# A fused attention and two-layer MLP kernel: selection rows made ahead of the decay, queries loaded once, another transfer price in the planner

## The chip, the cores and the metric

The kernel runs as one program on one core of one Trainium2 chip. The metric is device time in microseconds (us). The core has TensorE (PE in the profile; its weight loads, which overlap its matmuls, are PEld), VectorE (DVE), ScalarE (ACT), GpSimd (POOL) and SyncE (SP). SP issues every transfer of this kernel, in program order, and all of them share the core's 16 DMA engines.

## The reference, cut to what matters

```python
# q, k, v: [4, 8, 576, 64]; f: [4, 8, 576] in 0.8 .. 1.0
cum = np.cumsum(np.log(np.clip(f, 0.0001, 1.0)), axis=-1)
scores = q @ k.T / 8 + cum[..., :, None] - cum[..., None, :]   # causal mask
attn = softmax(scores) ;  x = (attn @ v) -> [2304, 512]
# layer 1: 512 -> 1024 -> 512
h = x @ w_in ;  solu = h * softmax(h) ;  ln = layernorm(solu) * g_ln
x = ln @ w_out
# layer 2: 512 -> 2048 -> 512
h = maximum(x @ w2_in, 0) ;  out = (h * h) @ w2_out
```

All tensors are float32. The kernel keeps that precision by splitting every large operand into a rounded high part and a low part (the difference), so that one product is three matmuls, or two with stacked rows.

## The kernel before

**Stages.** The 576 query rows of each of the 4 batches are cut into tiles of 128 rows (and one of 64), 20 tiles in all. For each tile and each of the 8 heads, `head` (L467) computes scores z (two matmuls, L488), their row minimum with the causal mask (DVE, L509), the exponential (ACT, L523) and the transposes of the result (PE, L543, copied out by a helper at L303), and `mix` (L549) multiplies two heads by v (PE, L564). When 128 rows of x are complete, `first` (L771) runs layer 1 on them (L786 to L788, then L863 and, in `out1`, L727 to L729) between later attention heads. Layer 2 runs at the end in blocks of 384 rows (`step`, L1044: L1059 to L1061 and L1089 to L1091). The weights come as raw words and are split on chip by `convert` (L619): a load (L629), then ACT L643, a scaling (L305 or L307), DVE L647 and L651, POOL L657, a rounding copy (L303 or L307) and the low part (L661, DVE or POOL). The weights of layer 1 are converted during the first attention tiles, those of layer 2 after the last one.

**The decay inside the score product.** A score is a product over 128 rows of `K1` and `Q1` plus one over 80 rows of `K2` and `Q2`. Rows 64 to 79 of `K2` hold the cumulated log of f (high and low part, 8 heads each), put there by small transfers (`auxrows`, L429). The same rows of `Q2` select the head with ones and zeros: `picks` (L398, L405) makes them once for each of the four `Q2` buffers, from the identity matrix alone. `picks` for the two buffers of the first tile carry the priority -6.9e6. For the first tile `c0` (the first 128 columns of the cumulated log, in two parts) goes straight into `K2`; the later tiles read it from a copy in DRAM, `cumd`.

**Operands.** `load` (L373) fetches k and q of a tile, for each half j of the heads, as 128 rows in which the 64 rows of the head dimension stand twice. `prep_k` (L409) rounds k into `K1` and writes its low part into `K2` (L421, on DVE or POOL, whichever the planner takes). `prep_q` (L443) writes the scaled, rounded q into `Q2` rows 0 to 63 and `Q1` rows 64 to 127, and its low part into `Q1` rows 0 to 63 (DVE, L456). k and q have one raw buffer for each half (`KN`, `QN`), so the load of the next tile waits until the last reader of its buffer is done.

**What sets the order.** Each step is given to a planner (`Plan`, L23) with a cost for each engine that may run it, a priority, and what it reads and writes. `Plan.lay` (L94) then lays out all steps before the program is built: of the steps that could start within 20 ns of the earliest it takes the one with the lowest priority number, chooses the engine, and so fixes the order on every engine's queue and on SP. On the chip an engine takes its queue strictly in this order; a step whose input is late holds all that stand behind it. The planner treats transfers as a sixth engine: 256 KB cost 800 ns, and `LAT` adds 910 to 1290 ns until the reader can start. `port=True` marks DVE steps that the planner keeps apart from POOL steps.

## Time and profile before

| | us |
|---|---|
| median of 3 timed runs | 898.15 (897.89 to 899.88) |
| the profiled execution, its own time | 895.01 |
| its span, first to last instruction | 892.9 |
| PE busy in the span | 841.4 (94%) |
| DVE, ACT, POOL busy | 459.4, 496.5, 294.1 |

The profiled execution lies 2.9 us below the lowest of the timed runs; 2.1 us of its time lie outside its span. Busy time of PE counts pipelined matmuls, so it is time in which PE had something in flight. The stages in time: attention and the conversion of the layer 1 weights to about 100 us, attention and layer 1 to about 450 us, conversion of the layer 2 weights beside the first blocks of layer 2 to about 570 us, and the rest of layer 2.

### The profile page before, as it was taken

Reading aid. Unit: us, or ns where it says so; the run is one execution under the profiler, and the core shown is the slowest. Engines: PE = TensorE matmul, PEld = TensorE weight load, DVE = VectorE, ACT = ScalarE, POOL = GpSimd, SP = SyncE. Lnnn points to the kernel's source line nnn. Section 1 sums busy time; section 2 is a strip of 40 time slices with the busy share of each in tenths; the row PEclk is TensorE's granted clock in tenths of the full one; section 3 lists DMA queues with packets and bytes.
Section 4 is the critical chain, followed back from the end, with each engine's and each line's share of the span. In section 5 each row is a group of like instructions: output and inputs, shape, how many; then the busy total and the mean of one; then the engine's idle time right before and its main releaser. Section 6 shows DMA issues by size and latency. Waiting matters only on the chain.

```text
span 892.9 us, 15185 instructions
## 1 busy us (share of the span) xinstructions
PE 841.4 (94%) x5360; PEld 728.5 (82%) x5360; DVE 459.4 (51%) x1139; ACT 496.5 (56%) x1286; POOL 294.1 (33%) x379
## 2 busy tenths in 40 slices
PE   3788899999999999999996999999999999999998
PEld 2556777888888888888875988899999999999997
DVE  6878666655655556655676789722222222222221
ACT  6889878666866667756675777523322222222222
POOL 6567756223521236211387788700000000000000
PEclk9979999999999999999998999999999999999999
DMA  6723335222511125010544644105002002000000
GB/s 219 233 86 126 106 108 157 83 59 66 171 48 37 59 67 165 29 42 24 162 145 132 223 140 131 48 1 177 36 0 72 36 1 71 36 1 1 36 0 36
DMA packets 55499, 75.26 MB, mean 84 GB/s; under 512 B 7456, under 2 KB 35104, under 8 KB 55424
## 3 DMA queue, kind: packets, MB, share of 16 engines
q1 hardware_dynamic: 55424, 74.30, 26.6%
q8 instruction: 42, 0.69, 0.3%
q14 instruction: 33, 0.27, 0.1%
HBM read 59.91 MB, written 14.30 MB: 83 GB/s over the span
## 4 chain that ended last, share of the span: by engine, by line
PE 77%; DVE 9%; DMA 5%; ACT 5%; issue 3%; POOL 2%; SPq 0%; POOLq 0%; DVEq 0%; ACTq 0%
PE pp L1059 6%; PE pp L1061 6%; PE pp L1060 6%; PE z L488 6%; PE pp L543 6%; PE xo L564 6%; PE pp L727 3%; PE hp L786 3%; PE hp L787 3%; PE hp L788 3%; PE pp L728 3%; PE pp L729 3%; PE hp L1089 2%; PE hp L1090 2%; PE hp L1091 2%
## 5 line engine op out<-in xcount | busy, mean ns | idle before, releaser
L1067 ACT ACTIVATE q<-pp 128x384 f32<-128x384 f32 x96 | 47.1, 491 | 223.1 <-PE pp L1061 221.0
L1070 DVE CAST q<-q 128x384 fp32r<-128x384 f32 x96 | 42.1, 438 | 243.4 <-PE xo L1091 92.3
L523 ACT ACTIVATE adj<-z,st 64x288 f32<-64x288 f32 (+9 forms) x192 | 94.9, 497 | 31.0 <-DVE st L509 29.3
L488 PE MATMUL z<-k,q 128*128 128x256 f32 (+17 forms) x384 | 95.1, 347 | 12.7 <-DVE q L456 9.1
L509 DVE CUSTOM_DVE_ANT_0 z<-z,maskb 128x128 f32<-128x128 f32 (+8 forms) x144 | 65.6, 464 | 52.8 <-PE z L488 49.9
L303 ACT COPY pt<-pp 128x384 f32<-128x384 f32 (+5 forms) x170 | 67.9, 420 | 39.0 <-PE pp L543 37.3
L543 PE MATMUL pp<-ident,adj 128*128 128x128 f32 (+1 forms) x480 | 78.7, 280 | 8.7 <-ACT adj L523 8.4
L727 PE MATMUL pp<-ln,woh 128*128 128x256 f32 x288 | 84.2, 292 | 2.3 <-ACT pt L303 2.3
L728 PE MATMUL pp<-ln,wol 128*128 128x256 f32 x288 | 80.8, 280 | 0.0
L729 PE MATMUL pp<-ln,woh 128*128 128x256 f32 x288 | 80.7, 280 | 0.0
L543 PEld LDWEIGHTS pp<-ident,adj 128*128 128x128 f32 (+1 forms) x480 | 52.8, 143 | 30.2 <-ACT adj L523 19.4
L488 PEld LDWEIGHTS z<-k,q 128*128 128x128 f32 (+3 forms) x384 | 58.4, 188 | 19.7 <-ACT q L305 7.9
L564 PE MATMUL xo<-pt,vn 128*64 128x128 f32 (+1 forms) x960 | 70.3, 278 | 3.8 <-ACT pt L303 3.1
L564 PEld LDWEIGHTS xo<-pt,vn 128*64 128x64 f32 x960 | 50.6, 140 | 23.6 <-issue 11.8
L786 PE MATMUL hp<-wih,xl 128*128 128x512 f32 x144 | 61.5, 427 | 2.2 <-ACT hp L825 1.8
L727 PEld LDWEIGHTS pp<-ln,woh 128*128 128x128 f32 x288 | 55.1, 191 | 5.3 <-ACT pt L303 2.6
L787 PE MATMUL hp<-wil,xh 128*128 128x512 f32 x144 | 57.2, 397 | 0.5 <-POOL wil L661 0.5
L788 PE MATMUL hp<-wih,xh 128*128 128x512 f32 x144 | 57.2, 397 | 0.0
L728 PEld LDWEIGHTS pp<-ln,wol 128*128 128x128 f32 x288 | 55.0, 191 | 0.5
L729 PEld LDWEIGHTS pp<-ln,woh 128*128 128x128 f32 x288 | 54.8, 190 | 0.0
L1069 ACT ACTIVATE q<-q 128x384 f32<-128x384 f32 x96 | 50.4, 525 | 2.5
L307 POOL TENSOR_SCALAR q<-qn 64x512 fp32r<-64x512 f32 (+1 forms) x43 | 28.0, 652 | 55.3 <-PE z L488 50.0
(470 smaller groups left out, 2233.5 us busy)
## 6 DMA issues: line engine op xcount, KB each, us to landing
x2d<-xc SPq DMA_DIRECT2D x72, 128.0 KB
kn<-in_k_dram SPq DMA_DIRECT2D x32, 256.0 KB
qn<-in_q_dram SPq DMA_DIRECT2D x32, 256.0 KB
vn<-in_v_dram SPq DMA_DIRECT2D x20, 256.0 KB
ln<-x2d SPq DMA_DIRECT2D x24, 192.0 KB
out_dram<-pt SPq DMA_DIRECT2D x18, 256.0 KB
pt<-in_moe_w_in_dram SPq DMA_DIRECT2D x17, 256.0 KB
ln<-in_moe_w_in_dram SPq DMA_DIRECT2D x8, 512.0 KB
```

The costliest lines, as they stand in the source:

```text
L303: nc.scalar.copy(dst(), src())
L488: nc.tensor.matmul(dst, lhsT=ql[0:r, p, 0:m], rhs=rhs, start=(g == 0), stop=(g == 1))
L509: nc.vector.tensor_tensor_reduce(out=z, in0=z, in1=maskb[0:m, o : o + e - a], scale=1.0, scalar=st[0:m, 0:1] if y else 3e38, op0=ALU.add, ...
L523: nc.scalar.activation(out=adj[0:m, c[1] : c[2]], in_=Z[c[0]][0:m, 0 : c[2] - c[1]], func=AF.Exp, bias=st[0:m, low : low + 1], scale=-1.0, ...
L543: nc.tensor.transpose(at(sk)[:, (c - g) * m : (c - g + 1) * m], adj[0:m, zc : zc + P], ident[0:m, 0:m])
L564: nc.tensor.matmul(XO[own[j], p, off : off + m], lhsT=VN[vslot[b, c]][:, (2 * p + j) * D : (2 * p + j + 1) * D], rhs=pts[j][:, c * m : (c ...
L727: nc.tensor.matmul(px, lhsT=woh[:, fc, w], rhs=lo, start=(fc == 0), stop=False)
L728: nc.tensor.matmul(px, lhsT=wol[:, fc, w], rhs=hi, start=False, stop=False)
L729: nc.tensor.matmul(px, lhsT=woh[:, fc, w], rhs=hi, start=False, stop=(fc == KF - 1))
L786: nc.tensor.matmul(HP[:, c], lhsT=XL[i][:, cc, :], rhs=wih[:, cc, w], start=(cc == 0), stop=False)
L787: nc.tensor.matmul(HP[:, c], lhsT=XH[i][:, cc, :], rhs=wil[:, cc, w], start=False, stop=False)
L788: nc.tensor.matmul(HP[:, c], lhsT=XH[i][:, cc, :], rhs=wih[:, cc, w], start=False, stop=(cc == KC - 1))
```

## The change

1. **Picking rows.** `picks` for the first tile's buffers gets priority -9.05e6, ahead of the steps on f (-9e6); that for the second tile's buffers goes from 5000 to 14000.
2. **First tile's parts.** The clip and the scan of the other 448 columns of f get -6.5e6 in place of -9e6 + 1. The low part of k of the first tile may run on DVE alone, no longer on POOL.
3. **Queries.** q is laid out once in DRAM: one load of 128 rows holds half 0 in rows 0 to 63 and half 1 in rows 64 to 127, into a single buffer `qn`. The steps of `prep_q` read the half that they need from it, across rows; the low part of half 1 takes the rounded value from `Q1`. The number of steps of `prep_q` is as before. The freed buffer (`q3`) serves layer 2 in place of the second `qn`.
4. **Planner.** 256 KB cost 1140 ns (230 GB/s; the other transfers in proportion), 500 ns more pass from a transfer to its reader, and a POOL step is not taken when a DVE step that needs the shared port, with a lower priority number by more than `DUE`, would start before the POOL step ends and lose more by waiting than POOL would.

```diff
-        dma=dict(pe=1000, dve=950, act=910, pool=950, dma=1290),
+        dma=dict(pe=1500, dve=1450, act=1410, pool=1450, dma=1790),
...
+                if e == "pool":
+
+                    end = c[0] + c[1].eng[e]
+                    x = [
+                        max(free["dve"], y.rdy["dve"]) for y in avail["dve"]
+                        if y.port and len(y.eng) == 1 and y.eng["dve"] and y.prio < c[1].prio - DUE
+                    ]
+                    if any(y < end and end - y > (y - c[0]) * WORTH for y in x):
+                        continue
...
-    QN = [new(f"qn{i}", [DM]) for i in range(2)]
+    QN = new("qn", [DM])
...
     def load_q(n, prio):
-        load("qn", QN, q, n, prio + 1)
+        T = tiles[n]
+        m, o = T["m"], HH * T["q0"]
+        pl.add(
+            dict(dma=1140 * m / P), lambda: nc.sync.dma_start(QN[:, 0 : HH * m], q[T["b"], :, o : o + HH * m]), prio + 1,
+            writes=["qn"],
+        )
...
-        s = pl.add(dict(dve=602, pool=1252) if i else dict(dve=602), fn, -6.9e6 if i == 0 else 5000, ["ident"], [("qa", i, j)], port=True)
+        s = pl.add(dict(dve=602, pool=1252) if i else dict(dve=602), fn, -9.05e6 if i == 0 else 14000, ["ident"], [("qa", i, j)], port=True)
...
-                dict(dve=67 + 1.045 * HH * m, pool=119 + 2.213 * HH * m), lo, prio + 2 * j, [("kn", j)] + hk, lk,
+                dict(dve=67 + 1.045 * HH * m, pool=119 + 2.213 * HH * m) if n else dict(dve=67 + 1.045 * HH * m),
+                lo, prio + 2 * j, [("kn", j)] + hk, lk,
...
-        for j in range(2):
+        raw = QN[:, 0 : HH * m].rearrange("p (h s) -> p h s", s=m)
+        for j, src in enumerate(own):
...
-            def lo(q1=q1, q2=q2, raw=raw):
+            def lo(src=src, q1=q1, hi=(q1 if j else q2)):
                 nc.vector.scalar_tensor_tensor(
-                    out=q1[LO, :, 0:m], in0=raw[LO], scalar=SC, in1=q2[LO, :, 0:m].bitcast(F32), op0=ALU.mult,
+                    out=q1[LO, :, 0:m], in0=raw[src], scalar=SC, in1=hi[src, :, 0:m].bitcast(F32), op0=ALU.mult,
...
-        pl.add(dict(dma=max(350, 2.844 * n)), words, prio - AHEAD, writes=[lk, hk])
+        pl.add(dict(dma=4.45 * n), words, prio - AHEAD, writes=[lk, hk])
...
-            ), -9e6 + y, ["f"], [("f", y)],
+            ), -9e6 + y * 2.5e6, ["f"], [("f", y)],
...
-            dict(dve=200 + 2 * n), scan, -9e6 + y, [("lf", y), "ones"] + ["cu0", ("xh", 0, 0)] * y, [f"cu{y}"]
+            dict(dve=200 + 2 * n), scan, -9e6 + y * 2.5e6, [("lf", y), "ones"] + ["cu0", ("xh", 0, 0)] * y, [f"cu{y}"]
```

The program is laid out anew, so the order shows what the numbers did. All names below: `adj` holds f and its logs at the start, `xh0` the two parts of c0, `q100`/`q200` and `q101`/`q201` are `Q1`/`Q2` of the first tile for half 0 and 1, `k20`/`k21` is `K2`, `ln` the raw words of w_in.

DVE at the start of the program, before:

```order
L1158 TENSOR_SCALAR adj0_30_97<-adj0_30_97 32x128
L1158 TENSOR_SCALAR adj0_30_97<-adj0_30_97 32x448
L1151 SCALAR_TENSOR_TENSOR adj2_32_99<-e_49_116,adj1_31_98 32x128
L1170 CAST xh0_45_112<-adj2_32_99 32x128
L1173 TENSOR_TENSOR xh0_45_112<-adj2_32_99,xh0_45_112 32x128
L1151 SCALAR_TENSOR_TENSOR adj2_32_99<-e_49_116,adj2_32_99,adj1_31_98 32x448
L456 SCALAR_TENSOR_TENSOR q100_12_79<-qn0_22_89,q200_16_83 64x512
L456 SCALAR_TENSOR_TENSOR q101_13_80<-qn1_23_90,q201_17_84 64x512
L405 TENSOR_TENSOR q200_16_83<-ident_0_67 16x512
L405 TENSOR_TENSOR q201_17_84<-ident_0_67 16x512
L1183 TENSOR_TENSOR pt1_51_174<-adj2_32_99,pt0_50_166 32x576
```

and after the change:

```order
L416 TENSOR_TENSOR q200_16_83<-ident_0_67 16x512
L416 TENSOR_TENSOR q201_17_84<-ident_0_67 16x512
L1175 TENSOR_SCALAR adj0_29_96<-adj0_29_96 32x128
L1175 TENSOR_SCALAR adj0_29_96<-adj0_29_96 32x448
L1168 SCALAR_TENSOR_TENSOR adj2_31_98<-e_48_115,adj1_30_97 32x128
L1187 CAST xh0_44_111<-adj2_31_98 32x128
L1190 TENSOR_TENSOR xh0_44_111<-adj2_31_98,xh0_44_111 32x128
L1168 SCALAR_TENSOR_TENSOR adj2_31_98<-e_48_115,adj2_31_98,adj1_30_97 32x448
L432 TENSOR_TENSOR k20_10_77<-kn0_20_87,k10_8_75 64x4x128
L468 SCALAR_TENSOR_TENSOR q100_12_79<-qn_22_89,q200_16_83 64x512
L432 TENSOR_TENSOR k21_11_78<-kn1_21_88,k11_9_76 64x4x128
L468 SCALAR_TENSOR_TENSOR q101_13_80<-qn_22_89,q101_13_80 64x512
L1200 TENSOR_TENSOR pt1_50_175<-adj2_31_98,pt0_49_162 32x576
```

The picking rows (L405, now L416) went from behind the queries' low parts to the front of the queue, ahead of the clip of f; the two low parts of k (L432), which POOL held before, now stand between the scan of the 448 columns and the first row minimum.

SP, from the first load of w_in (`ln`) to the third, before:

```order
L629 DMA ln0_50_168<-in_moe_w_in_dram 128x1024
L1130 DMA cumd_59<-pt0_50_166 32x576
L379 DMA kn0_20_87<-in_k_dram 128x512
L379 DMA qn0_22_89<-in_q_dram 128x512
L1130 DMA cumd_59<-pt1_51_174 32x576
L379 DMA kn1_21_88<-in_k_dram 128x512
L379 DMA qn1_23_90<-in_q_dram 128x512
L395 DMA vn1_25_92<-in_v_dram 128x512
L629 DMA ln0_50_168<-in_moe_w_in_dram 128x1024
L629 DMA ln1_51_234<-in_moe_w_in_dram 128x1024
```

and after the change:

```order
L644 DMA ln0_49_166<-in_moe_w_in_dram 128x1024
L1147 DMA cumd_59<-pt0_49_162 32x576
L388 DMA kn0_20_87<-in_k_dram 128x512
L1147 DMA cumd_59<-pt1_50_175 32x576
L396 DMA qn_22_89<-in_q_dram 128x512
L388 DMA kn1_21_88<-in_k_dram 128x512
L406 DMA vn1_24_91<-in_v_dram 128x512
L644 DMA ln0_49_166<-in_moe_w_in_dram 128x1024
L644 DMA ln1_50_238<-in_moe_w_in_dram 128x1024
```

One q load in place of two stands between the first and the second load of w_in.

ACT, in the second half of the first tile, around the second chunk of w_in (the `ACTIVATE ln` from L643, now L658), before:

```order
L523 ACTIVATE adj1_31_98,su0_40_107<-z0_117,st0_36_103 128x128
L523 ACTIVATE adj2_32_99,su0_40_107<-z1_118,st1_37_104 128x128
L303 COPY pt0_33_100<-pp2_123 128x128
L303 COPY pt1_34_101<-pp0_121 128x128
L643 ACTIVATE ln0_50_168<-ln0_50_168 128x512
L305 ACTIVATE ln0_50_168<-ln0_50_168 128x512
L303 COPY pt2_35_102<-pp1_122 128x128
L523 ACTIVATE adj0_30_97,su0_40_107<-z0_117,st2_38_105 128x128
L523 ACTIVATE adj1_31_98,su0_40_107<-z1_118,st3_39_106 128x128
```

and after the change:

```order
L538 ACTIVATE adj2_31_98,su0_39_106<-z1_117,st1_36_103 128x128
L314 ACTIVATE q110_14_81<-qn_22_89 64x512
L312 COPY pt0_32_99<-pp2_122 128x128
L312 COPY pt1_33_100<-pp0_120 128x128
L538 ACTIVATE adj0_29_96,su0_39_106<-z0_116,st2_37_104 128x128
L312 COPY pt2_34_101<-pp1_121 128x128
L658 ACTIVATE ln0_49_166<-ln0_49_166 128x512
L312 COPY pt0_32_99<-pp2_122 128x128
L314 ACTIVATE q111_15_82<-qn_22_89 64x512
L538 ACTIVATE adj1_30_97,su0_39_106<-z1_117,st3_38_105 128x128
```

Two of the exponentials (`adj`) stood behind the second chunk of w_in before, one does now, and two scalings of q (L314) moved here from POOL.

## Rows read from the trace of the kernel before

**Rows 1.** The page, part 1: busy us, share, instructions of PE.

```profile
PE 841.4 (94%) x5360; PEld 728.5 (82%) x5360; DVE 459.4 (51%) x1139; ACT 496.5 (56%) x1286; POOL 294.1 (33%) x379
```

**Rows 2.** Stages: busy us by engine, granted clock, DMA share, GB/s.

```profile
0.00:20.00 20.00, 7.40 (x29) 5.14 (x30) 14.03 (x29) 12.44 (x32) 14.32 (x25) 1.00 0.68 212
20.00:40.00 20.00, 15.30 (x79) 10.81 (x79) 14.82 (x36) 17.43 (x47) 10.17 (x11) 1.00 0.73 228
40.00:60.00 20.00, 15.17 (x75) 10.92 (x76) 17.17 (x32) 16.36 (x40) 11.30 (x8) 0.66 0.44 140
...
100.00:150.00 50.00, 46.83 (x388) 38.11 (x387) 32.86 (x101) 37.97 (x124) 30.86 (x42) 0.97 0.42 126
...
300.00:350.00 50.00, 50.00 (x430) 41.41 (x431) 28.10 (x92) 35.63 (x110) 21.93 (x27) 1.00 0.32 100
...
450.00:500.00 50.00, 39.12 (x216) 34.24 (x215) 37.49 (x74) 32.46 (x86) 39.44 (x52) 0.93 0.40 128
```

**Rows 3.** What PE waited for, 0 to 150 us: total, times, longest.

```profile
PE z L488 <- DVE q L456: 9.1, 2, 8.0
...
PE z L488 <- DVE q L405: 1.7, 1, 1.7
```

**Rows 4.** Timeline of the start: start, us, engine, line, operation, [idle before].

```profile
1.50 0.29 POOL masks.py:199 TENSOR_SCALAR_AFFINE_SELECT ident<-ident 128x128 f32<-128x128 f32 x1
...
5.26 4.30 POOL L421 TENSOR_TENSOR k<-kn,k 64x512 fp32r<-64x512 f32 x2
...
6.15 2.29 DVE L456 SCALAR_TENSOR_TENSOR q<-qn,q 64x512 fp32r<-64x512 f32 x2
...
8.45 3.10 DVE L405 TENSOR_TENSOR q<-ident 16x512 fp32r<-16x512 f32 x2
...
11.58 0.75 DVE L1183 TENSOR_TENSOR pt<-adj,pt 32x576 fp32r<-32x576 f32 x1
12.26 0.28 DVE L509 CUSTOM_DVE_ANT_0 z<-z,maskb 128x128 f32<-128x128 f32 x1
...
12.87 0.68 DVE L405 TENSOR_TENSOR q<-ident 16x512 fp32r<-16x512 f32 x1
```

**Rows 5.** The chain of waits, 0 to 27 us: start us, us, what.

```profile
2.72 0.67 DVE adj L1158 x2
...
4.72 1.50 DVE adj L1151
...
14.16 7.00 DMA ln<-in_moe_w_in_dram
...
23.96 1.38 DVE wil L661
...
26.08 0.78 PE z L488 x2
```

**Rows 6.** Timeline of ACT, up to 22 us.

```profile
5.55 0.63 ACT L305 ACTIVATE q<-qn 64x512 fp32r<-64x512 f32 x1
...
18.21 0.42 ACT L303 COPY pt<-pp 128x128 f32<-128x128 f32 x2
...
21.19 0.66 ACT L643 ACTIVATE ln<-ln 128x512 f32<-128x512 f32 x1 [2.56 <-DMA ln<-in_moe_w_in_dram]
```

**Rows 7.** Timeline of SP, three of its issues.

```profile
14.16 0.91 SPq L629 DMA_DIRECT2D ln<-in_moe_w_in_dram  x2
...
29.55 0.46 SPq L1130 DMA_DIRECT2D gcol<-in_moe_g_ln_dram  x1
35.22 0.34 SPq L379 DMA_DIRECT2D kn<-in_k_dram  x1
```

**Rows 8.** Stages 14 to 21.2 us and 41.5 to 55.5 us.

```profile
14.00:21.20 7.20, 6.26 (x26) 3.95 (x25) 3.33 (x12) 4.11 (x18) 4.33 (x5) 1.00 0.85 266
...
41.50:55.50 14.00, 10.76 (x46) 7.82 (x43) 13.12 (x24) 12.00 (x27) 8.62 (x6) 0.51 0.45 145
```

**Rows 9.** Timeline of PE: the last of the eight L786 of the first tile.

```profile
64.67 0.40 PE L786 MATMUL hp<-wih,xl 128*128 128x512 f32 x1
```

More of the change, by code (lines that the diff above doesn't have):

```diff
@@ L371, in tile_kernel, with load_k @@
     vslot = {}
-    def load(nm, dst, src, n, prio):
+    def load_k(n, prio):
         T = tiles[n]
@@ L768, in out1 @@
                 wk = [("x2d", a, cc, 2 * blk + r) for r in range(2)]
-                pl.add(dict(dma=365), store(a), prio, [(nm, i, r) for r in range(2)], wk)
+                pl.add(dict(dma=570), store(a), prio, [(nm, i, r) for r in range(2)], wk)
     def first(x):
@@ L977, in tile_kernel @@
     small = [f"vn{i}" for i in range(NV)] + [f"q{a}{i}{j}" for a in (1, 2) for i in range(2) for j in range(2)]
-    small += ["kn0", "kn1", "qn0", "qn1"]
+    small += ["kn0", "kn1", "qn", "q3"]
     skeys = {f"vn{i}": [("vn", i)] for i in range(NV)}
     for i in range(2):
-        skeys[f"kn{i}"], skeys[f"qn{i}"] = [("kn", i)], [("qn", i)]
+        skeys[f"kn{i}"] = [("kn", i)]
         for j in range(2):
@@ L1111, in step @@
                 pl.add(
-                    dict(dma=728), lambda o=o, r0=r0: nc.sync.dma_start(out[r0 : r0 + P, :], o()), prio + DOWN,
+                    dict(dma=1140), lambda o=o, r0=r0: nc.sync.dma_start(out[r0 : r0 + P, :], o()), prio + DOWN,
                     [("o", oi)], [("out", r0)],
```

29 lines of the change are left out of this document (15 added, 14 removed).

## The prediction

> **What bounds the kernel now.** I read the busy times first: PE has something in flight for 94% of the span [rows 1]. A share of the span hides stages, so the stages came next [rows 2]; a row names PE, PEld, DVE, ACT and POOL in this order. From 300 to 350 us PE is busy for 50.00 of 50 us and no other engine for over 36: there only less matmul work would help, and the change leaves the matmuls as they are. From 0 to 60 us PE is busy for 7.40, 15.30 and 15.17 of 20 us each, so 22.1 us are idle, and in the third stage the granted clock was 0.66. From 100 to 150 us 3.2 us are idle, from 450 to 500 us 10.9. So what the change can give lies in the first 60 us, what it can spoil also at 450 to 500 us, and what is won early is kept: PE has no gap between in which it could be lost.
>
> Then I asked what PE waited for in the early part [rows 3]: the low part of q, L456, twice (8.0 us at the very start and 1.1 us later), and 1.7 us for the picking rows, L405. The timeline of the start and the chain of waits show how these come about [rows 4, 5]: after f has landed, DVE alone does the clip, the scans, the q low parts, the picking rows and the split of the log, until the first row minimum at 12.26 us. The second wait ends the first tile: the chain goes through a 7.00 us load of w_in, its conversion on ACT, its low part on DVE (1.38 us) and the q low part behind it, to the second tile's first scores at 26.08 us.
>
> **The start.** The picking rows need the identity, which POOL ends at 1.50 + 0.29 = 1.79 us [rows 4]. One alone takes 0.68 us, so two end at about 3.25 us. f is ready at 2.72 us [rows 5], so the clip starts some 0.5 us later than now. From its start to the end of the second scan it takes 4.72 + 1.50 - 2.72 = 3.50 us [rows 5], which gives 6.75 us. Four steps of 512 columns follow, two low parts of k (on POOL before, 4.30 us for both) and two of q; at 0.68 us they end at 9.5 us, and with the split of the log (0.75 us) the first row minimum starts at 10.2 us in place of 12.26: -2.0 us. The second scan, though its priority is later now, still stands where it stood, since nothing else is ready for DVE then. The clean sum is one end. At the other, POOL holds DVE up as it does now: the two picking rows took 3.10 us beside POOL's low part of k and picking row, against 1.36 us for two alone [rows 4], 1.7 us too much; paid once more, it leaves -0.3 us. I take -1.5, nearer the clean end, because POOL's two long steps are gone from there. The small transfers of c0 into K2 are issued 0.5 us later than now, some 5 us into the span; K2 is first used at about 9.5 us, so they have 4 us. If they took the 7.00 us of a load of w_in under full queues [rows 5], the start would gain nothing.
>
> The Trainium skill's SBUF — State Buffer, in its section on the two separate sides of SBUF, speaks against this part: a DVE instruction with two SBUF inputs and a GpSimd instruction that reads SBUF lock each other out for a whole instruction. The stretched picking rows agree [rows 4]. By that rule the copies of k and q that POOL now makes in a row could hold up the four low parts on DVE as well; with the whole 1.7 us paid, the start would be worth -0.3 us, and my sum below would give 894.4.
>
> **ACT in the first tile.** Between the first and the last exponential the order now has three scalings of q and one rounding of w_in on ACT, and no longer two scalings of w_in: two steps more at 0.63 us [rows 6], +1.2 us. The bounds are 0 (if they fall into waits) and +1.3.
>
> **The second chunk of w_in.** ACT was done at 18.63 us and then stood for 2.56 us, until that chunk had landed [rows 6]; two exponentials of the first tile were queued behind it. Its load was issued at 14.16 us [rows 7], behind the second copy to cumd, which waits for the split of the log: this moves up with the start, by 1.5 us. Ahead of it 10 loads of 256 KB stood beside the first chunk, and now 8: 0.52 MB less at the 266 GB/s of that stretch [rows 8] are 2.0 us. So it lands at about 17.7 us and not 21.2, ahead of ACT, which comes to it at 18.6 - 1.5 + 1.2 = 18.3 us or later, and only one exponential still stands behind it: -2.6 us. Bounds: that whole wait, and 0.
>
> **The second tile's scores.** The q low part that they wait for stood on DVE behind w_in's low part (1.38 us) [rows 5]; in the new order it stands ahead. The PE wait of 1.1 us [rows 3] goes; bounds -1.1 and 0.
>
> **The rest of w_in.** SP issued nothing from 30.0 to 35.2 us [rows 7], because a load of k waited for its buffer and chunks of w_in stood behind it. In the new order chunks 7 and 8 have no k load directly ahead, but chunk 6 has; and q takes 1.5 us less of the queues per tile. The best case gives most of the 5.2 us back (-4), the worst adds a wait for chunk 6 (+3 by the same row). I take -1.0.
>
> **At no cost.** The second tile's picking rows (0.68 us on DVE or POOL) stay within DVE's free time (14.0 of 20 us busy); otherwise 0.7 us. One q buffer for both halves makes the next load wait for the last of its readers; it is issued more than a tile ahead of use, and a load under full queues took 7.00 us, and the first tile alone lasts from the row minimum at 12.26 to 26.08 us [rows 4, 5], which covers it; otherwise PE would wait at each tile. The reading across rows adds no instruction. At 450 to 500 us loads wait for buffers, so that their price in the planner changes only places in the order; DVE (37.5) and POOL (39.4 of 50 us) stay the bound [rows 2]. I take 0, with 2 us either way.
>
> **Sum.** -1.5 + 1.2 - 2.6 - 1.1 - 1.0 = -5.0 us. Against the profiled execution's own 895.01 us that is 890.0. The runs that count have their median 3.1 us higher, for a reason that the profile doesn't show; the difference applied to it gives 898.15 - 5.0 = 893.15, rounded to 893.2. With the bounds of the first 26 us (-7.0 to +1.0) and the rest I give this case 889.5 to 896.
>
> **The rivals.**
> *The gain is spent at the weights.* From 40 to 60 us DVE is busy for 17.2 of 20 us and ACT for 16.4 [rows 2]; if the splitting of w_in sets the pace up to there and not the start, the attention that starts earlier only stands longer at layer 1. For it: the chain of conversions. Against it: those engines are idle for 6 and 8 of the first 20 us, and the chunks come earlier. It leaves about -1: 897.1.
>
> *Layer 1 is put ahead of its weights: slower.* In the new order of PE the eighth L786 group of the first tile stands behind 44 score matmuls, 50 before. It ran at 64.67 us [rows 9]; from the second tile's first scores at 26.08 us (the 17th) that is 38.6 us for 34 matmuls, 1.13 us each, so six are worth 6.8 us. PE takes its queue in order. If the loads keep the last chunk where it is, the scores behind the group stand still for up to 6.8 us, and with the 4.0 us that the first tile wins, 2.8 us are lost: 901.0. It turns to a loss where the last chunk is split less than 6.8 us earlier than now and the engines had nothing else to do. For it: chunk 6 behind k loads. Against it: the steps that split the chunks moved ahead by the same three heads on ACT and DVE, so the order is the planner's trade of one work for the other.
>
> *The clock stays up: more gain.* From 41.5 to 55.5 us the granted clock was 0.51, the 1.2 GHz level, with PE busy for 10.8 of 14 us, after a stretch in which PE stood idle for a quarter of the time [rows 2, 8]. With fewer waits it may stay at 2.4 GHz. Up to 5.4 us of PE time would go, but DVE was busy for 13.1 of the 14 us, so I count 3, and 2 for the best case of w_in: 888.2.
>
> **How the numbers follow.** Chances: the forecast 0.50, spent at the weights 0.20, layer 1 ahead of its weights 0.17, the clock 0.13. 0.2% (1.8 us) is about what a measurement of this kernel can tell from no change. Faster by more: 0.49 of the forecast, 0.13 and 0.02 of the second case, 0.64. Within: 0.19. Slower: 0.17. The range for 8 in 10 reaches from 886 to 901: it leaves out half of the slower case and a part of the clock's. The likeliest case's own range is 889.5 to 896.
>
> **What would show it.** The first row minimum at 10.2 to 11.5 us; no wait of ACT for the second chunk of w_in; the second tile's scores at 21 to 23 us in place of 26.08; 22.1 us of PE idle in the first 60 us down to about 17; PE busy without a gap from 150 to 450 us as now. I am wrong if PE stands at L786 for weights for more than 2 us in sum, if DVE steps at 4 to 10 us take over 1.2 us each, or if the stretch from 450 to 570 us is longer by more than 2 us.

## The result, and the profile after

The changed kernel takes 887.59 us (median of 4 runs, 886.61 to 887.74), the kernel before 898.23 us (4 runs, 897.89 to 899.88): a ratio of 0.9876, 95% interval 0.9859 to 0.9893. That is 10.6 us, against 5.0 forecast; the time lies inside the range of 886 to 901. Profiled execution against profiled execution it is 895.01 to 886.61 us, so 8.4; the other 2.2 us are the difference between a profiled execution and a median, 3.2 us before and 1.0 after. In 75 later executions the kernel before has a median of 897.2 us; against that the gain would be 9.6 us.

Line numbers after are 9 to 17 higher (L303 is L312, L1059 is L1076). The page's busy line and the stages of the changed kernel, in the columns of [rows 1] and [rows 2]:

```profile
PE 842.8 (95%) x5360; PEld 727.6 (82%) x5360; DVE 466.2 (53%) x1141; ACT 496.1 (56%) x1282; POOL 295.1 (33%) x381
```

```profile
0.00:20.00 20.00, 7.91 (x31) 5.51 (x31) 15.44 (x35) 12.86 (x36) 15.30 (x26) 1.00 0.66 209
20.00:40.00 20.00, 16.54 (x82) 11.46 (x81) 15.69 (x34) 17.05 (x45) 11.14 (x9) 1.00 0.68 209
40.00:60.00 20.00, 14.25 (x85) 9.56 (x84) 17.57 (x35) 19.46 (x46) 12.26 (x13) 0.91 0.36 110
100.00:150.00 50.00, 47.96 (x390) 38.70 (x388) 35.41 (x109) 39.47 (x127) 29.91 (x40) 0.90 0.38 113
...
450.00:500.00 50.00, 42.86 (x254) 37.76 (x253) 41.07 (x82) 37.12 (x105) 42.45 (x54) 0.93 0.52 156
```

No engine works less by more than 1 us. PE is busy for 3.7 us more from 450 to 500 us than in [rows 2]. Stages of fixed length shift against the work, so I cut both traces at the same points of PE's work: the 37th group of L786, the 241st of L727 and the 113th of L1059. Before, then after (columns as in [rows 2]):

```profile
0.00:157.47 157.47, 124.69 (x849) 94.64 (x849) 113.87 (x288) 127.22 (x349) 101.11 (x131) 0.93 0.48 149
157.47:442.72 285.25, 285.24 (x2315) 245.60 (x2313) 168.92 (x503) 192.49 (x532) 83.56 (x113) 1.00 0.25 75
442.72:602.97 160.25, 145.21 (x766) 128.80 (x765) 113.21 (x210) 96.76 (x251) 109.43 (x136) 0.98 0.38 120
```

```profile
0.00:152.77 152.77, 125.14 (x848) 95.47 (x849) 118.08 (x290) 126.34 (x342) 100.55 (x131) 0.93 0.44 136
152.77:438.48 285.71, 285.23 (x2315) 244.91 (x2314) 170.00 (x506) 193.21 (x532) 83.96 (x113) 1.00 0.22 66
438.48:594.78 156.30, 145.95 (x766) 128.18 (x765) 114.74 (x208) 96.73 (x252) 110.61 (x138) 0.98 0.41 126
```

The first stretch is 4.7 us shorter, the second 0.5 longer, the third 4.0 shorter; the rest is alike within 0.2. Below they are *early*, *middle* and *weights*. PE's busy time is the same in each to within 0.8 us; its idle time (length less busy) fell early from 32.8 to 27.6 us and in weights from 15.0 to 10.4.

What changed at the weights of layer 2 stands in the waits of ACT for transfers from 430 to 600 us (total, times, longest). Before, 7.9 us in all:

```profile
ACT pt L305 <- DMA pt<-in_moe_w_out_dram: 2.1, 1, 2.1
...
ACT x L305 <- DMA x<-in_moe_w_in_dram: 1.8, 2, 1.2
...
ACT pt L305 <- DMA pt<-in_moe_w_in_dram: 1.2, 4, 0.5
ACT adj L305 <- DMA adj<-in_moe_w_in_dram: 1.2, 2, 0.9
...
ACT adj L643 <- DMA pt<-in_moe_w_in_dram: 0.9, 1, 0.9
...
ACT adj L305 <- DMA adj<-in_moe_w_out_dram: 0.7, 1, 0.7
```

After, 1.6 us:

```profile
ACT x L314 <- DMA x<-in_moe_w_in_dram: 1.0, 1, 1.0
...
ACT pt L314 <- DMA pt<-in_moe_w_in_dram: 0.4, 2, 0.3
...
ACT xw L658 <- DMA pt<-in_moe_w_out_dram: 0.2, 1, 0.2
```

The longest of before, in ACT's timeline (columns as in [rows 6]), with what stood behind it:

```profile
474.04 0.43 ACT L305 ACTIVATE pt<-pt 128x256 uint32<-128x256 uint32 x1 [2.09 <-DMA pt<-in_moe_w_out_dram]
474.38 0.39 ACT L303 CAST k<-adj 128x256 fp32r<-128x256 f32 x1
474.67 0.48 ACT L1067 ACTIVATE q<-pp 128x384 f32<-128x384 f32 x1
```

ACT takes its queue in order. Behind a load that has not landed stand roundings of weights whose data are there (L303) and the first step of layer 2's activation (L1067). PE's three largest waits from 430 to 600 us, before and then after:

```profile
PE z L1089 <- ACT xw L643: 4.1, 2, 3.6
PE z L1089 <- ACT adj L643: 4.0, 1, 4.0
PE z L1089 <- DVE kn L1073: 3.2, 3, 1.7
```

```profile
PE z L1106 <- DVE kn L1090: 3.8, 4, 1.4
PE hp L1106 <- DVE qn L1090: 2.3, 4, 1.1
PE pp L1076 <- ACT k L312: 2.1, 3, 1.1
```

The two that the profile puts down to ACT's conversion of weights (L643), 8.1 us together, are gone. These rows do not show that late loads made them. L643 writes nothing that L1089 reads. Both waits end right after DVE's step `kn`, which works on the result of L1067 and of the square behind it (L1069):

```profile
477.07 1.07 DVE L1073 TENSOR_TENSOR kn<-q,q 128x384 fp32r<-128x384 f32 x1
...
478.29 0.71 PE L1089 MATMUL z<-k,kn 128*128 128x512 f32 x1 [4.04 <-ACT adj L643]
...
486.76 0.95 DVE L1073 TENSOR_TENSOR kn<-q,q 128x384 fp32r<-128x384 f32 x1
...
487.86 0.47 PE L1089 MATMUL z<-k,kn 128*128 128x512 f32 x1 [3.59 <-ACT xw L643]
```

The first began at 478.29 - 4.04 = 474.25 us, when PE had ended the products that L1067 reads; ACT had its late load by 474.04 us. So it was, for the most part, the way of one result from PE over ACT and DVE back to PE, with nothing else laid out for PE meanwhile. The experiments show that the planner's numbers for transfers shorten PE's idle time in weights; in what way they do it stays open.

### The profile page after: what moved, and what is told of

Same layout as the page of the kernel before. It is cut to its first block, busy times and chain, and to the rows that moved or that the text cites. A ratio compares the mean times of both kernels' runs of the same rounds, so it can differ in the third digit from the quotient of the medians.

```text
span 884.8 us, 15092 instructions
## 1 busy us (share of the span) xinstructions
PE 842.8 (95%) x5360; PEld 727.6 (82%) x5360; DVE 466.2 (53%) x1141; ACT 496.1 (56%) x1282; POOL 295.1 (33%) x381
## 3 DMA queue, kind: packets, MB, share of 16 engines
q1 hardware_dynamic: 52544, 69.58, 25.2%
HBM read 55.19 MB, written 14.30 MB: 79 GB/s over the span
## 4 chain that ended last, share of the span: by engine, by line
PE 78%; DVE 7%; ACT 7%; POOL 4%; issue 3%; DMA 2%; SPq 0%; ACTq 0%; POOLq 0%; DVEq 0%
PE pp L558 6%; PE z L503 6%; PE xo L579 6%; PE pp L1078 6%; PE pp L1077 6%; PE pp L1076 6%; PE hp L801 4%; PE hp L803 3%; PE hp L802 3%; PE pp L742 3%; PE pp L743 3%; PE pp L744 3%; PE hp L1106 2%; PE hp L1107 2%; PE hp L1108 2%
## 5 line engine op out<-in xcount | busy, mean ns | idle before, releaser
L1087 DVE CAST q<-q 128x384 fp32r<-128x384 f32 x96 | 40.2, 419 | 241.8 <-PE xo L1108 92.3
L558 PE MATMUL pp<-ident,adj 128*128 128x128 f32 (+1 forms) x480 | 81.2, 284 | 15.0 <-ACT adj L538 14.5
L312 ACT COPY pt<-pp 128x256 f32<-128x256 f32 (+5 forms) x169 | 68.5, 421 | 41.5 <-PE pp L558 38.2
L558 PEld LDWEIGHTS pp<-ident,adj 128*128 128x128 f32 (+1 forms) x480 | 54.2, 146 | 36.1 <-ACT adj L538 23.8
L579 PE MATMUL xo<-pt,vn 128*64 128x128 f32 (+1 forms) x960 | 70.2, 280 | 0.2 <-ACT pt L312 0.2
L579 PEld LDWEIGHTS xo<-pt,vn 128*64 128x64 f32 x960 | 50.6, 141 | 20.3 <-issue 14.3
L801 PE MATMUL hp<-wih,xl 128*128 128x512 f32 x144 | 61.1, 425 | 1.9 <-ACT hp L840 1.0
L316 POOL TENSOR_SCALAR q<-qn 64x512 fp32r<-64x512 f32 (+1 forms) x39 | 26.1, 669 | 44.2 <-PE z L503 42.2
```

The costliest lines, as they stand in the source:

```text
L312: nc.scalar.copy(dst(), src())
L558: nc.tensor.transpose(at(sk)[:, (c - g) * m : (c - g + 1) * m], adj[0:m, zc : zc + P], ident[0:m, 0:m])
L579: nc.tensor.matmul(XO[own[j], p, off : off + m], lhsT=VN[vslot[b, c]][:, (2 * p + j) * D : (2 * p + j + 1) * D], rhs=pts[j][:, c * m : (c ...
L801: nc.tensor.matmul(HP[:, c], lhsT=XL[i][:, cc, :], rhs=wih[:, cc, w], start=(cc == 0), stop=False)
```

## The experiments

17 other kernels ran, and the kernel before once more (o_before_again, one execution); the table gives all, and the parts below say what each is. Each ratio is against the kernel before on the same chip. *Lost* is span x (1 - mean granted clock), the median over a kernel's executions: the time that TensorE would have saved had its clock never been at the lower of its two levels (1.2 and 2.4 GHz), if it was busy then. *Rest* is the span less that, also a median. For the kernel before both come from the 75 later executions beside the experiments, on four chips. The last five columns come from the profiled execution: idle time of PE early and in weights, lost time early, change of the length of weights against before, and ACT's waits for transfers from 430 to 600 us. Lost time early is summed over slices and good to 0.2 us. A diff shows the lines that matter; where a number changes, its fellows for other transfers change in proportion.

| kernel | median | ratio [95%] | lost | rest | idle early | lost early | idle weights | length | ACT |
|---|---|---|---|---|---|---|---|---|---|
| before | 898.2 | 1 | 17.0 | 878.6 | 32.8 | 10.1 | 15.0 | 0 | 7.9 |
| after | 887.6 | 0.9876 [0.9859, 0.9893] | 15.9 | 870.0 | 27.6 | 10.1 | 10.4 | -4.0 | 1.6 |
| o_before_again | 897.6 | | 15.2 | 880.2 | 33.7 | 10.2 | 14.5 | +0.9 | 9.7 |
| a_first | 895.5 | 0.9982 [0.9953, 1.0011] | 11.2 | 880.8 | 33.7 | 5.1 | 14.6 | +1.4 | 10.0 |
| b_q_once | 891.4 | 0.9929 [0.9906, 0.9952] | 12.0 | 877.4 | 30.0 | 10.3 | 14.0 | -1.2 | 10.8 |
| c_prices | 889.9 | 0.9908 [0.9872, 0.9944] | 12.4 | 875.4 | 30.7 | 13.8 | 11.0 | -6.6 | 1.2 |
| d_pool_rule | 894.4 | 0.9955 [0.9931, 0.9978] | 14.3 | 877.9 | 31.1 | 12.1 | 14.8 | -0.3 | 10.8 |
| e_no_prices | 895.2 | 0.9984 [0.9962, 1.0005] | 13.4 | 878.8 | 31.7 | 6.9 | 15.1 | +1.2 | 8.7 |
| h_q_twice | 893.7 | 0.9964 [0.9950, 0.9979] | 15.1 | 876.2 | 30.9 | 15.3 | 9.8 | -3.5 | 2.2 |
| g_after_no_first | 889.3 | 0.9913 [0.9891, 0.9935] | 11.1 | 876.4 | 30.2 | 10.3 | 10.6 | -4.2 | 1.6 |
| f_after_no_pool | 888.8 | 0.9903 [0.9886, 0.9921] | 12.0 | 874.7 | 26.6 | 6.8 | 12.9 | +1.0 | 0.3 |
| m_prices_l2 | 893.6 | 0.9960 [0.9935, 0.9985] | 14.7 | 876.9 | 32.4 | 11.8 | 13.4 | -2.4 | 4.0 |
| n_lat_only | 885.1 | 0.9882 [0.9845, 0.9919] | 8.8 | 875.9 | 31.3 | 5.2 | 9.1 | -5.0 | 4.0 |
| w_lat_1000 | 890.3 | 0.9930 [0.9902, 0.9957] | 14.2 | 874.7 | 32.5 | 6.7 | 13.5 | -1.3 | 3.0 |
| u_lat_q_once | 891.5 | 0.9947 [0.9927, 0.9968] | 16.4 | 873.3 | 31.0 | 11.9 | 11.8 | -3.6 | 4.1 |
| s_after_lat_only | 888.6 | 0.9912 [0.9883, 0.9940] | 14.6 | 873.3 | 26.7 | 11.9 | 9.0 | -5.2 | 4.3 |
| t_after_price_only | 887.2 | 0.9891 [0.9862, 0.9921] | 11.5 | 874.2 | 28.4 | 6.9 | 13.4 | -1.8 | 5.2 |
| p_half | 914.5 | 1.0213 [1.0176, 1.0251] | 18.3 | 895.4 | 37.7 | 12.0 | 19.9 | +6.9 | 25.6 |
| r_high | 916.4 | 1.0227 [1.0181, 1.0273] | 25.2 | 889.1 | 39.7 | 27.5 | 13.9 | -1.4 | 0.0 |
| j_other_order | 898.6 | 1.0022 [0.9992, 1.0051] | 17.1 | 879.1 | 32.4 | 11.9 | 16.5 | +1.3 | 8.2 |

**One part alone, on the kernel before.** The start (parts 1 and 2):

```diff
-... -6.9e6 if i == 0 else 5000, ["ident"], ...
+... -9.05e6 if i == 0 else 14000, ["ident"], ...
-                dict(dve=67 + 1.045 * HH * m, pool=119 + 2.213 * HH * m), lo, ...
+                dict(dve=67 + 1.045 * HH * m, pool=119 + 2.213 * HH * m) if n else dict(dve=67 + 1.045 * HH * m), lo, ...
-            ), -9e6 + y, ["f"], [("f", y)],
+            ), -9e6 + y * 2.5e6, ["f"], [("f", y)],
```

> The kernel before with only the picking rows' priorities, the priorities of f's second part and the first tile's low part of k on DVE. Where the change gained: 4.8 us up to layer 1's fifth group of rows (the 37th L786, at 157.5 us before), and 4 us more between 443 us and 603 us, where the weights of layer 2 are converted. Theory 'each part by itself': the first row minimum comes 1 us earlier (11.3 us), 1 to 2 us of that are left at 157.5 us, nothing changes after 443 us: ratio 0.998 to 0.999. Theory 'any new order can gain or lose at layer 2's conversion': the stretch from 443 to 603 us differs by 1 us or more either way though nothing of this change acts there.

Its interval includes 1. The early stretch is 3.1 us shorter in the profile, yet PE is idle for 0.9 us more in it: what fell is the time lost to the clock, 10.1 to 5.1 us. The start itself came as forecast, with the first row minimum at 10.84 us, 1.4 earlier, but was not kept: up to 160 us ACT waits for w_in for 7.0 us in all, 3.5 before.

```profile
10.84 0.28 DVE L509 CUSTOM_DVE_ANT_0 z<-z,maskb 128x128 f32<-128x128 f32 x1
```

```profile
ACT ln L643 <- DMA ln<-in_moe_w_in_dram: 7.0, 2, 4.3
```

One load of the queries (part 3):

```diff
-    QN = [new(f"qn{i}", [DM]) for i in range(2)]
+    QN = new("qn", [DM])
```

> The kernel before with only the queries loaded once. Theory 'the second chunk of w_in' (my step): ACT's wait of 2.56 us for that chunk shrinks to under 1 us and the second tile's scores come 2 to 3 us earlier; 2 to 3 us are left at the 37th L786; nothing after 443 us: ratio 0.997. Rival 'the prices made the order that avoids the wait': ACT still waits for over 2 us, under 1 us is gained. Theory 'any new order': 443 to 603 us differs by 1 us or more.

It reads 4.7 MB less (59.91 to 55.19 MB from HBM) and gains 0.7%; early idle time falls by 2.8 us. ACT's wait for the second chunk of w_in falls from 2.56 to 0.52 us, and the second tile's first scores come at 24.43 us, 1.65 earlier, a little less than the 2 to 3 expected:

```profile
18.70 0.68 ACT L649 ACTIVATE ln<-ln 128x512 f32<-128x512 f32 x1 [0.52 <-DMA ln<-in_moe_w_in_dram]
```

```profile
24.43 0.80 PE L494 MATMUL z<-k,q 128*128 128x256 f32 x2
```

The planner's numbers for transfers (the first half of part 4):

```diff
-        dma=dict(pe=1000, dve=950, act=910, pool=950, dma=1290),
+        dma=dict(pe=1500, dve=1450, act=1410, pool=1450, dma=1790),
-        pl.add(dict(dma=max(350, 2.844 * n)), words, prio - AHEAD, writes=[lk, hk])
+        pl.add(dict(dma=4.45 * n), words, prio - AHEAD, writes=[lk, hk])
```

> The kernel before with only the planner's transfer prices (1140 ns for 256 KB, 500 ns more to the reader). Theory 'prices': with prices near what the chip does, the order at layer 2's conversion is better, 3 to 4 us less from 443 to 603 us, and 1 to 3 us less up to 157.5 us since ACT is no longer sent to chunks that have not landed: ratio 0.993 to 0.995. Theory 'any new order': the stretch from 443 to 603 us differs by 1 us or more either way, as in the other kernels. Theory 'POOL rule': nothing from 443 us on.

They alone shorten weights by 6.6 us and take ACT's waits there to 1.2 us: my step that put them at nothing is refuted. Early they lengthen the way by 0.9 us, with 2.1 us less idle time and about 3.5 us more lost to the clock.

The rule for POOL:

```diff
+                    if any(y < end and end - y > (y - c[0]) * WORTH for y in x):
+                        continue
```

> The kernel before with only the rule that holds a POOL step back for a DVE step on the shared port. Theory 'POOL rule': DVE (75 to 85% busy) and POOL (80%) bound layer 2's conversion, fewer stretched DVE steps there give 2 to 4 us from 443 to 603 us: ratio 0.996. Theory 'prices': nothing there. Theory 'any new order': 1 us or more either way.

Early idle falls by 1.7 us; weights stay as they were, where 2 to 4 us were expected.

**One part undone, on the changed kernel.** Old numbers for transfers:

```diff
-        dma=dict(pe=1500, dve=1450, act=1410, pool=1450, dma=1790),
+        dma=dict(pe=1000, dve=950, act=910, pool=950, dma=1290),
-        pl.add(dict(dma=4.45 * n), words, prio - AHEAD, writes=[lk, hk])
+        pl.add(dict(dma=max(350, 2.844 * n)), words, prio - AHEAD, writes=[lk, hk])
```

> The changed kernel with the old transfer prices and latencies in the planner. Theory 'prices': the 6.6 us that the prices alone won from 443 to 603 us are missing, so that stretch is 2 to 5 us longer than in the changed kernel (156.3 us), and the start keeps what it won: about 891 to 893 us. Theory 'any new order': the stretch differs from both kernels by 1 to 3 us either way, without a sign that follows from the prices.

Without them nearly all of the gain is gone, more than expected; ACT waits for 8.7 us again, and weights are as long as before.

Queries loaded twice:

```diff
-    QN = new("qn", [DM])
+    QN = [new(f"qn{i}", [DM]) for i in range(2)]
```

> The changed kernel with the queries loaded twice as before. Two things to tell apart. Gain: by my second step 2 to 3 us of the first 157 us come from the missing q loads, so 889 to 891 us. Spread: runs of before lie 8.6 us apart, and of the two kernels with q loaded twice 6.3 and 8.9, of those with q once 1.3 and 1.1 (changed). Theory 'the second q load makes the runs differ', by transfers that land later or earlier around the first tiles: runs spread by over 4 us. Rival 'the order of the start does': they stay within 2 us.

It costs 7.9 us of the 10.6 (0.9964 against 0.9876 of 898). Weights keep their gain; early, 3.3 us more idle time and in this execution 5.2 us more lost to the clock. Its ten runs lie within 1.8 us, so the second load of the queries is not what spreads the runs of before (892.1 to 901.4 us).

The old start, and no rule for POOL:

```diff
-... -9.05e6 if i == 0 else 14000, ["ident"], ...
+... -6.9e6 if i == 0 else 5000, ["ident"], ...
```

> The changed kernel with the start of the kernel before (row picks and first tile's parts where they were, ScalarE and GpSimd sharing them). Theory (TensorE's time to a fixed point of its work is idle time plus time lost at half clock; the idle times of the parts add, within 2.5 us, the lost clock does not): the start alone added 1.0 us of idle time by 157 us, so without it the idle time there is 26 to 29 us (27.6 in the changed kernel), the point at 157 us differs from the changed kernel's by idle plus lost clock within 1.5 us, 443 to 603 us stays 2 to 6 us shorter than before; time 884 to 893 us, the clock deciding. Rival (my step on the start: it is worth 1.5 us of waits): idle time there 1.5 us or more higher than in the changed kernel, time 888 to 891 us.

```diff
-                    if any(y < end and end - y > (y - c[0]) * WORTH for y in x):
-                        continue
```

> The changed kernel without the rule that keeps GpSimd from steps that are wanted early. Theory (as in the run beside it): the rule alone took 1.6 us of idle time by 157 us, so without it 27 to 32 us of idle time there (27.6 in the changed kernel), the point at 157 us differs by idle plus lost clock within 1.5 us; 443 to 603 us stays 2 to 6 us shorter than before; time 886 to 894 us. Rival (the rule changes nothing that ends a wait): idle time within 0.5 us of the changed kernel's and the time within 1 us of it.

Here I had let go of my step on the start, and it held: without the start PE is idle for 2.6 us more early, above the 26 to 29 expected. The point at its end moves by 0.9 us only; by the account that a stretch changes as PE's idle time and the lost time do together, it would have moved by 2.8. About 0.8 us of the rest has a reason: twelve of `mix`'s products (L579 after; sixteen take 1.02 us) stand ahead of the point in the changed kernel and behind it here, as in c, f, s, u and w. Against before, the account misses the early length by less than 2 us, but for f_after_no_pool (2.6) and r_high (3.9). Without the rule idle time is 1.0 us less early, against the expectation and hardly more than chance; weights are 0.9 us longer than before, with 2.1 us less idle time and 8.5 us lost to the clock, 3.4 before. That profile is the slowest of its four executions.

**Which number does it at the weights?** The new prices for layer 2's transfers alone, and the kernel before once more:

```diff
+                ("2r", ri), ("2w", wi), ("w2", fc, c, hf), ld=4.45 * 256,
-                pl.add(dict(dma=546), fn, prio, rk, [("x2", e, a, cc)])
+                pl.add(dict(dma=850), fn, prio, rk, [("x2", e, a, cc)])
```

> The kernel before with the new transfer prices only for layer 2's loads (weights, x, outputs); latencies, layer 1 and k, q, v as before. The order is that of before up to the last attention tiles. Theory 'prices of layer 2's loads': 3 to 6.6 us less from 443 to 603 us, nothing before: ratio 0.993 to 0.997. Theory 'any new order': -2 to +2 us. Theory 'latencies': under 1 us, since the 500 ns to the reader are not in it.

> The kernel before, unchanged, for another profiled execution. The first profiled one took 895.0 us, while the median is 898.2 to 898.7. Theory 'early part': an execution that takes longer loses the difference before 157 us, where ACT waits for w_in. Theory 'clock': it loses it where the granted clock is low for longer (40 to 60 us, 470 to 495 us), at whichever stage. Theory 'everywhere': each stretch is longer in proportion.

The prices there are worth 2.4 us of weights, less than the 3 expected. The kernel before took 897.55 us; against its first profile early is 1.3 us longer and weights 0.9, PE's idle time differs by 0.9 and 0.5 us, and ACT's waits by 1.8: so much is chance between two executions, and every other kernel has one profile.

Four more: the latency alone; on the kernel before, about half the prices and 500 ns off the latency; on the changed kernel, 1.4 times its prices and 500 ns more latency; and on the kernel before, a change of one cost without meaning, which moves only the order of layer 2:

```diff
-        dma=dict(pe=1000, dve=950, act=910, pool=950, dma=1290),
+        dma=dict(pe=1500, dve=1450, act=1410, pool=1450, dma=1790),
```

> The kernel before with one line of the change alone: a landed load is taken by the planner to release its readers 500 ns later; the prices stay the old ones. Theory (it is the price of a transfer in the planner, not the lateness added behind it, that keeps ScalarE's queue off loads that have not landed): ScalarE's waits for transfers at 430 to 600 us stay at 8 to 12 us, as in the kernel before (7.9) and in the four runs with old prices (8.7 to 10.8); the stretch from the 241st first-layer piece to the 113th last product stays within 1.5 us of the kernel before; time 895 to 899 us. Rival (lateness of either kind does it): ScalarE's waits fall to 4 us or less, the stretch is 2.5 to 6.5 us shorter, time 890 to 894 us.

```diff
-        pl.add(dict(dma=max(350, 2.844 * n)), words, prio - AHEAD, writes=[lk, hk])
+        pl.add(dict(dma=max(200, 1.5 * n)), words, prio - AHEAD, writes=[lk, hk])
```

> The kernel before with every transfer at a little over half its old price in the planner (256 KB in 400 ns) and the landing taken to release 500 ns earlier: the opposite of the change's last part. Theory (prices that are too low send ScalarE to loads that have not landed): its waits for transfers at 430 to 600 us rise above 10 us, the stretch from the 241st first-layer piece to the 113th last product is 1 to 5 us longer than in the kernel before, time 898 to 904 us. Rival (any other order of layer 2's stage is better than this one, whatever the price): the stretch is shorter by 2 us or more, time 890 to 896 us.

```diff
-        pl.add(dict(dma=4.45 * n), words, prio - AHEAD, writes=[lk, hk])
+        pl.add(dict(dma=6.2 * n), words, prio - AHEAD, writes=[lk, hk])
```

> The changed kernel with every transfer priced 1.4 times higher again in the planner (256 KB in 1600 ns) and 500 ns more behind each. Theory (all that was to be had is ScalarE's wait for loads, and 1.6 us of it are left at 430 to 600 us): within 2 us of the changed kernel, 886 to 890 us, ScalarE's waits there at 0 to 3 us. Rival (the price has a best value near what the trace moves, and above it the loads are put too late or other work too early): slower than the changed kernel by 3 us or more, 891 to 897 us, with ScalarE or TensorE waiting for weights again.

```diff
-        pl.add(dict(act=371), ...
+        pl.add(dict(act=391), ...
```

> The kernel before with one cost in the planner altered without meaning: the ScalarE step that squares in the second layer's activation is put down as 391 ns in place of 371. Prices of transfers are untouched; only the order of layer 2's stage changes. Theory (the gain at 443 to 603 us comes from the prices): that stretch within 1.5 us of the kernel before, ScalarE's waits for transfers there at 6 to 12 us, time 895 to 900 us. Rival (the gain there is the luck of another order, the prices only one way to draw it): the stretch is shorter by 2.5 us or more with ScalarE's waits as long as before, time 890 to 894 us.

My theory (price, not lateness) fell: lateness (the latency behind a transfer) alone shortens weights by 5.0 us and halves ACT's waits. One other order alone does nothing (j_other_order), and numbers that are too low do the reverse, beyond what was expected: under p_half ACT waits for 25.6 us, led by

```profile
ACT pt L305 <- DMA pt<-in_moe_w_in_dram: 5.9, 11, 1.1
```

and each of the three stretches is longer, by 5.4, 7.8 and 6.9 us. r_high was slower than either expectation allowed. ACT waits for no transfer in weights, but early is 20.4 us longer; its row for 20 to 40 us:

```profile
20.00:40.00 20.00, 12.77 (x58) 8.71 (x59) 11.80 (x27) 11.76 (x30) 9.75 (x10) 1.00 0.45 133
```

moves 133 GB/s and not 209, and PE, DVE and ACT are busy for 3.8, 3.9 and 5.3 us less than in the changed kernel. I take it that transfers priced above what the chip needs are laid out late, and the work on them too; the rows show the idle engines, not the planner's reason, nor whether price or lateness did it. The mean clock of its early stretch is 0.85.

**Do the parts add?** Lateness or price alone inside the changed kernel; on the kernel before, lateness with one query load, and 1000 ns of lateness in place of 500:

```diff
-        pl.add(dict(dma=4.45 * n), words, prio - AHEAD, writes=[lk, hk])
+        pl.add(dict(dma=max(350, 2.844 * n)), words, prio - AHEAD, writes=[lk, hk])
```

> The changed kernel with the old prices of transfers and the new lateness behind each. Theory (lateness keeps ScalarE's queue off loads that have not landed, the prices add nothing): ScalarE's waits for transfers at 430 to 600 us at 1 to 5 us, the stretch from the 241st first-layer piece to the 113th last product 3 to 6 us shorter than in the kernel before, time 882 to 889 us. Rival (the price does the work, and the run with lateness alone was a lucky order): waits of 8 us or more, time 893 to 898 us, as with neither.

```diff
-        dma=dict(pe=1500, dve=1450, act=1410, pool=1450, dma=1790),
+        dma=dict(pe=1000, dve=950, act=910, pool=950, dma=1290),
```

> The changed kernel with the new prices of transfers and the old lateness behind each. Theory (lateness is what counts): ScalarE's waits for transfers at 430 to 600 us at 6 us or more, the stretch there within 2 us of the kernel before, time 892 to 898 us. Rival (either does it, since both make the planner take a load as landed later): waits of 4 us or less, the stretch 2 to 6 us shorter, time 885 to 891 us.

```diff
-        dma=dict(pe=1000, dve=950, act=910, pool=950, dma=1290),
+        dma=dict(pe=1500, dve=1450, act=1410, pool=1450, dma=1790),
-    QN = [new(f"qn{i}", [DM]) for i in range(2)]
+    QN = new("qn", [DM])
```

> The kernel before with the new lateness and the queries loaded once; old prices, old start. Theory (loading the queries once takes 4.7 MB off the transfers of the first 440 us, which is worth something only where TensorE or ScalarE waits for a load; lateness has taken those waits): within 2 us of lateness alone, 883 to 887 us. Rival (the two add up, as each alone is worth 6 us and more): 877 to 881 us.

```diff
-        dma=dict(pe=1000, dve=950, act=910, pool=950, dma=1290),
+        dma=dict(pe=2000, dve=1950, act=1910, pool=1950, dma=2290),
```

> The kernel before with 1000 ns more lateness behind each transfer in place of the 500 ns, prices old. Theory (what is left of ScalarE's waits at 430 to 600 us is 4 us with 500 ns, and r_high's loss comes from its prices, which fill the planner's transfer queue, not from its lateness): waits at 0 to 3 us, time 882 to 888 us. Rival (lateness beyond what the chip shows makes the planner put work behind loads that are long there, and is what cost r_high its time): 893 to 915 us.

Either number inside the changed kernel keeps most of the gain. s_after_lat_only met its expectation in full; t_after_price_only falls between its two (waits of 5.2 us, weights 1.8 us shorter, 887.2 us). u_lat_q_once met neither expectation: against lateness alone its *rest* is 2.6 us lower, but it loses 7.6 us more to the clock. The last run falls between its two: ACT's waits shrink to 3.0 us, but PE's idle time in weights is 13.5 us, so more lateness is not better.

**What follows.** In weights the idle time of PE sorts the kernels by the planner's numbers: 14.0 to 16.5 us with the old ones (seven profiles: before, o_before_again with 14.5, a, b, d, e, j), 9.0 to 13.9 with either raised (twelve), 19.9 with lower ones. The two groups nearly touch, and not every raise is worth much: price alone leaves 13.4 us (m, t) and 1000 ns more lateness than before 13.5 and 13.9 (w, r_high), while 500 ns more leave 9.0 to 12.9 with or without the price (n, s, u, c, after, g, h, f). ACT's waits do not set this idle time alone: r_high and f_after_no_pool have 0.0 and 0.3 us of them and 13.9 and 12.9 us idle, n_lat_only and s_after_lat_only 4.0 and 4.3 and only 9.1 and 9.0. Early, r_high and p_half aside, it is 28.4 us or less only in the four kernels that hold one query load, a raised number and the start together (after, s, t, f), and 30.0 to 33.7 in all others, each part alone among them. And two kernels with the same time have it for different reasons: lateness alone has a *rest* 5.9 us above that of the change, and 7.1 us less lost. The first stretch of the two differs in its clock (n_lat_only; the change has 0.93):

```profile
0.00:151.60 151.60, 120.28 (x849) 92.14 (x849) 119.43 (x292) 126.46 (x347) 99.14 (x131) 0.97 0.51 154
```

No kernel beats the change by more than the intervals.

## Why the prediction was wrong, step by step

**The step that failed: 450 to 500 us at nothing.** The prediction said that loads wait for buffers there, so that their price changes only places in the order, and that DVE and POOL stay the bound. Weights gave 4.0 us, twice the 2 us allowed either way. The planner's numbers alone gave 6.6 us there (c_prices), and without them the gain there was gone (e_no_prices), so places in the order were the very thing that counted. Nor were DVE and POOL full: from 450 to 500 us they are busy for 41.07 and 42.45 us after the change, 37.49 and 39.44 before. A hint was in the trace of before, ACT's waits for transfers at 430 to 600 us (7.9 us, 1.6 after); I read the busy times there, not the waits. They are a sign and not shown to be the cause: the two longest waits of PE do not follow from them.

**The start, -1.5, bounds -2.0 to -0.3.** It gave 0.9: the first row minimum at 11.32 us in place of 12.26. DVE's timeline:

```profile
1.83 1.38 DVE L416 TENSOR_TENSOR q<-ident 16x512 fp32r<-16x512 f32 x2 [0.98 <-POOL ident masks.py:199]
3.24 0.61 DVE L1175 TENSOR_SCALAR adj<-adj 32x128 f32<-32x128 f32 x2
...
6.45 1.03 DVE L432 TENSOR_TENSOR k<-kn,k 64x512 fp32r<-64x512 f32 x1
7.41 0.67 DVE L468 SCALAR_TENSOR_TENSOR q<-qn,q 64x512 fp32r<-64x512 f32 x1
8.01 1.09 DVE L432 TENSOR_TENSOR k<-kn,k 64x512 fp32r<-64x512 f32 x1
9.13 1.48 DVE L468 SCALAR_TENSOR_TENSOR q<-qn,q 64x512 fp32r<-64x512 f32 x1
10.64 0.75 DVE L1200 TENSOR_TENSOR pt<-adj,pt 32x576 fp32r<-32x576 f32 x1
11.32 0.28 DVE L524 CUSTOM_DVE_ANT_0 z<-z,maskb 128x128 f32<-128x128 f32 x1
```

POOL's steps beside the four low parts:

```profile
5.41 1.54 POOL L316 TENSOR_SCALAR q<-qn 64x512 fp32r<-64x512 f32 x1
...
7.01 1.56 POOL L316 TENSOR_SCALAR q<-qn 64x512 fp32r<-64x512 f32 x1
...
9.03 1.03 POOL L416 TENSOR_TENSOR q<-ident 16x512 fp32r<-16x512 f32 x1
```

The picks and the clip came as worked out (3.24 us, 0.5 later). Three of the four low parts were stretched, 4.27 us for all against 4 x 0.68: 1.5 us of the 1.7 that I took only in part. Each of the three ended 0.53 to 0.55 us after a POOL step did (6.95, 8.57 and 10.06 us). The fourth was not stretched, but the POOL step beside it was: 1.56 us, where POOL's first scaling of q took 0.61. In a_first, with POOL out of the way for three of the four, they took 0.67 us each and the forecast of the start came true. The rule of the Trainium skill that I had weighed against this step (SBUF — State Buffer, the section on the two separate sides of SBUF: a DVE instruction with two SBUF inputs and a GpSimd instruction that reads SBUF lock each other out) agrees with these rows.

**Up to the second tile, -4.0 with the start.** Its first scores ran at 23.39 us in place of 26.08, so -2.7. The second chunk of w_in was issued at 13.23 us, not 14.16, and ACT came to it without a wait, as the prediction has it, but later, behind the query scalings that moved to ACT:

```profile
13.23 0.90 SPq L644 DMA_DIRECT2D ln<-in_moe_w_in_dram  x2
...
19.93 0.68 ACT L658 ACTIVATE ln<-ln 128x512 f32<-128x512 f32 x1
...
23.39 1.22 PE L503 MATMUL z<-k,q 128*128 128x256 f32 x4
```

So the mechanism was right (one query load alone takes most of that wait of ACT away, b_q_once), and its terms together were too large by 1.3 us, 0.6 of them in the start. The prediction's lower bound for these 26 us, -7.0, is a slip: its own terms (-2.0, 0, -2.6, -1.1) give -5.7.

**The rest of w_in, -1.0.** The last of the first tile's L786 groups, now L801, came 8.2 us earlier (64.67 us in [rows 9]):

```profile
56.46 0.48 PE L801 MATMUL hp<-wih,xl 128*128 128x512 f32 x1
```

of which 3.5 were given back until 157 us: early in all -4.7, against the sum's -5.0. So the sum came out right for its stretch by luck, with two misses of 1.3 and 1.0 us that offset each other. Both of its cases came in part: SP issued chunk 6 of w_in at 32.91 us, 4.0 later than before, but the last chunk by 35.8 us (41.40 before). The 22.1 us of idle time in the first 60 us fell to 21.3 only, not to 17: PE's gain came between 60 and 157 us. PE waits for exponentials (L558 for `adj`) for 14.5 us up to 150 us, 8.4 before: I take it that it runs ahead more and then waits more for ACT:

```profile
PE pp L558 <- ACT adj L538: 14.5, 13, 3.1
PE z L503 <- DVE q L468: 8.2, 1, 8.2
...
PE hp L802 <- POOL wil L676: 0.9, 1, 0.9
PE hp L801 <- POOL wih L316: 0.8, 1, 0.8
```

**The rivals.** PE waited for weights of layer 1 (`wil`, `wih`) for 1.7 us in all, and the last group came 8.2 us earlier, so neither of the two rivals at those weights occurred. The clock stayed up where that rival has it (0.91 from 40 to 60 us, 0.66 before) and fell elsewhere (0.90 from 100 to 150 us, 0.97 before): 10.1 us were lost early before and after. So its 888.2 lies near the measured time by chance.

**The median.** I carried the 3.1 us between profiled execution and median over unchanged; after the change it is 1.0. The 5.6 us that the sum missed are these 2.2 and the 4.0 at the weights, less 0.3 early and 0.5 in the middle; 0.2 remain. About half of the 2.2 has a place in the runs: the profiled execution of before lost 14.3 us to the clock, its later ones 17.0 in the median; for the change it is 14.2 and 15.9. The rest is open.
